# A fused attention, expert and gated layer: the last expert and the wide stage written out as one list of steps for three engines

## The chip, the core and the metric

The kernel runs on one core of a Trainium2 chip. Its engines work side by side, each on its own queue, in order: TensorE (PE in the profile; its weight loads are PEld), VectorE (DVE), ScalarE (ACT), GpSimd (POOL) and SyncE (SP), which here issues transfers. The metric is the device time of one execution in microseconds (us). The profile is that of one execution on this core.

## What is computed

Attention in a window of 128 positions gives 2304 tokens of 512 numbers. Each token goes to the one of eight experts that its gate picks (two layers, 512 to 1024 to 512). The result goes through a gated layer that all tokens share, 512 to 1536 to 512; this is the wide stage.

```
attn = softmax(scale*q@k.T + bias, inside a window of 128) @ v      # 4 batches, 8 heads, 576 positions
e_idx = argmax(x @ w_gate, axis=1)
for e in range(8):
    h = np.maximum(x[mask] @ w1[e], 0.0)
    out[mask] = gate_w[mask, None] * eom[mask, e, None] * (h @ w2[e])
g = x @ w_gate2;  val = x @ w_val                                   # x is now out
y = ((g * sigmoid(g)) * val) @ w_out
```

The weights of the gated layer come as 64-bit numbers and are narrowed to 32 bits in the kernel.

## The kernel before

Three stages follow each other: attention, the experts, the wide stage. A matmul takes 32-bit numbers as a high part and a low part (high = a rounded copy, written by ACT; low = number minus high, a subtraction by DVE or POOL), and every product is three passes: high by high, high by low, low by high (`PASSES`).

**Experts.** The experts are sorted by how many tokens they have; expert p takes `CAPS[p]` columns (384 for the first, 256 for the last two). Each has 16 steps: eight blocks `m` of the first layer, then eight blocks `kk` of the second. After every step `behind_step` turns some weights that will be needed later into high and low parts, by the table `plan`: rows of the next experts and, from step 40 on, halves of the wide stage's weights, which `narrow` puts together (two ACT operations, lines 327 and 329, then two DVE merges, lines 335 and 340). The results of an expert go to `ys`, a matrix in DRAM with one column for each token; they are copied by ACT and stored by transfers that ACT issues (`store_y`, for the seventh expert `store_whole`). The columns of `ys` that no expert may write are set to zero by four transfers in the attention stage (`zero_cols`, line 265).

**Wide stage.** The 2304 columns of `ys` are taken in three pairs of units (a unit is 384 columns), and each pair in 12 steps, one for each 128 columns of gate and value, so s runs from 0 to 35. A scheme with seven products in place of eight gives gate and value of both units: seven sums of the columns (`x_sum`, `x_high`, `x_low`) meet seven sums of the weights (`w_sum`, made by `sums`; `w_hi`; `w_lo`). In step s PE runs `product` 0 to 6, six matmuls of 384 columns each, into two banks `pa` and `pb`; and between them `wide_out(s - 2, ...)`, six groups of three matmuls of 512 columns, which multiply the finished activations of step s-2 with the output weights into six further banks. Beside PE, one step holds:

- ACT copies the banks (`s_p5`, `s_p1`, `s_u2`), two sigmoids, the high parts of the activations (`high`) and of the next step's weights (`w_hi`).
- DVE adds `v1`, `v2` and `g1` (lines 1377, 1395, 1408), multiplies (lines 1320, 1321, 1326, 1327), makes the low parts of the activations (`low`, line 1254) and three of the seven low parts of the weights (line 1080).
- POOL makes the other four low parts (line 1080) and the four sums of the weights (line 1063).

In the first pair, pair 0, each step also narrows two blocks of output weights (`out_weights`, `out_halves`: ACT, two merges each on DVE, the low parts on POOL, line 1303) and stores them to DRAM (`wo_s`), from which the later pairs load them again (`out_reload`). At the end of a pair the columns of the next are loaded (`load_unit`, line 967), summed (DVE and POOL, line 1027) and split (ACT line 1040, DVE line 1044), each 768 wide; and the finished rows of the pair leave by scatters that POOL issues (`wide_store`). For pair 0 this preparation lies in the steps of the last expert (`wide_early`).

What sets the order: inside `manual_schedule` every engine runs its instructions in the order in which the code issues them. So the loops above are the order. In a step of the wide stage the four merges stand on DVE ahead of `v2`:

```
if pr == 0:
    out_halves(G)
    out_weights(f)
TT(out=v2, in0=bank_a, in1=s_p5, op=ALU.add)
```

The seventh product adds into `bank_a`, so it waits until `v2` has read that bank. And at the end of the seventh expert:

```
if p == E - 2:
    for i in range(2):
        xraw[i] = new_slot((128, 2048), F32)
        load_unit(i)
...
store_whole(p, o, n)
```

The load of the first columns stands in front of the store of the seventh expert's results; the store goes to the same matrix at a column known only on the chip, and so waits until the load has landed, on ACT's queue.

Of the kernel before, what the change touches and what calls it, by code (L numbers as in the profile page):

```python
# [46 lines left out]
e2 E14.0 K13.1 r2 x11* S14.1 k2 D5 V12.0 H12 w2 H13 V12.1 D2 Q16.1 C14.1 H14 G5 v17 y0 y1 y2 y3 N5 p13.0 t7 M14.1 L11* l5 t4  # L47
# [5 lines left out]
x17 X15 L15* G8 X14 r4 a8 l8 a6 a7 k4 F8 D12 t17 f8 g5 D13 e5 w5 D15 r5 t16 b5 D14 X17 k5 X16 D17 D16  # L53
""".split()
# [3 lines left out]
def attn_moe_glu_kernel(ctx, tc, q, k, v, w_gate, w_ogate, w1, w2, w2_gate, w2_val, w2_out, out, caps=CAPS):  # L58
# [9 lines left out]
    WU = 384  # L68
# [56 lines left out]
    with ExitStack():  # L125
# [135 lines left out]
        LOW = caps[0] + min(caps)  # L261

        def zero_cols(d):
            w = next(x for x in range(RW, 0, -1) if (NT - LOW) % x == 0)
            nc.sync.dma_start(
                out=ys[d * 128:d * 128 + 128, LOW:NT].rearrange("p (a w) -> p a w", w=w),
                in_=zrow[:, 0:w].unsqueeze(1).to_broadcast([128, (NT - LOW) // w, w]),
            )

# [54 lines left out]
        def narrow(t, act=False, out=None):  # L324
# [3 lines left out]
            if act:  # L328
                nc.scalar.activation(  # L329
                    out=lo, in_=lo.bitcast(U32), func=AF.Copy, scale=2.0 ** -29 * (1 - 2.0 ** -11),  # L330
                    bias=2.0 ** -8 - 0.5,
                )
            else:
                nc.vector.tensor_scalar(out=lo, in0=lo, scalar1=29, scalar2=None, op0=ALU.logical_shift_right)
# [9 lines left out]

        loaded, halves, lows, n_rows = [], [], [], [0]
# [25 lines left out]
        def w_item(eng):  # L371
# [9 lines left out]
            else:  # L381
# [3 lines left out]
                narrow(t, True, wraw[fp][:, :, AT[name[0]][kk], :])  # L385
# [317 lines left out]
        def w_low(i):  # L703
# [5 lines left out]
            "q": load_qk, "v": load_v, "z": zero_fill, "y": zero_cols, "T": turn_in, "Q": keep_in, "S": scores, "C": select, "M": biased, "E": expo, "N": norm, "P": turn_p, "p": keep_p, "K": parts, "V": values, "x": keep_o, "t": turn_x, "X": rows_x, "D": place,  # L709
# [35 lines left out]
        tbl = wB[0].tile([128, 2048], F32, tag="wx", name="tbl", bufs=NX)  # L745

# [219 lines left out]
        def load_unit(u):  # L966
            nc.sync.dma_start(
                out=grid(xraw[u % 2], KD, WU), in_=ys[:, u * WU:u * WU + WU].rearrange("(k p) n -> p k n", p=128)
            )

# [12 lines left out]

        def store_whole(p, o, n):
            y = grid(raw_tile(), KD, n)
            for d in range(KD):
                nc.scalar.activation(out=y[:, d, :], in_=o[d][:, 0:n], func=AF.Copy)
            nc.scalar.dma_start(
                out=ys[:, bass.ds(off_reg[p], n)].rearrange("(k p) n -> p k n", p=128), in_=y
            )  # L990
# [18 lines left out]
        xset, wring, sbuf, wsum = [], [], [], []  # L1009
# [4 lines left out]
        def x_src(i):  # L1014
            r0, r1 = xraw
            return {0: sbuf[0], 1: r0[:, 0:UW], 2: sbuf[0], 3: sbuf[1], 4: sbuf[1], 5: r0[:, UW:2 * UW],
                    6: r1[:, UW:2 * UW]}[i] if sbuf else None

        def x_sum(i, eng):
            r0, r1 = xraw  # L1020
            a, b, op = {
                0: (r1[:, 0:UW], r1[:, UW:2 * UW], ALU.add),
                3: (sbuf[0], r0[:, 0:UW], ALU.subtract),
                2: (r0[:, UW:2 * UW], sbuf[1], ALU.subtract),
                4: (r0[:, 0:UW], r1[:, 0:UW], ALU.subtract),
            }[i]
            eng.tensor_tensor(out=x_src(i), in0=a, in1=b, op=op)
# [5 lines left out]
        def x_parts(i):  # L1033
            if i < 6:
# [3 lines left out]
        def x_high(i):  # L1038
            for src, hi, lo in x_parts(i):
                nc.scalar.activation(out=hi, in_=src, func=AF.Copy)  # L1040

        def x_low(i, eng):
            for src, hi, lo in x_parts(i):
                eng.tensor_tensor(out=lo, in0=src, in1=hi, op=ALU.subtract)
# [5 lines left out]
        def w_sum(s, i):  # L1050
# [3 lines left out]
        def sums(s, which):  # L1054
            if s >= NS:
                return
            g1, v2, g2, v1 = (w_raw(s, i) for i in range(4))
            for i in which:
                a, b, op = {
                    0: (v1, g1, ALU.subtract), 2: (v2, v1, ALU.subtract), 1: (w_sum(s, 2), g1, ALU.add),  # L1060
                    3: (g2, w_sum(s, 1), ALU.subtract),
                }[i]
                nc.gpsimd.tensor_tensor(out=w_sum(s, i), in0=a, in1=b, op=op)  # L1063

        def w_at(s, j):
            g = 7 * s + j
            return wring[g // 4 % 3][:, g % 4]

        def w_src(s, j):
            return w_sum(s, {0: 0, 3: 1, 4: 2, 6: 3}[j]) if j in (0, 3, 4, 6) else w_raw(s, {1: 0, 2: 1, 5: 2}[j])  # L1070

        def w_hi(s, *js):
            for j in js:
                if s < NS:
                    nc.scalar.activation(out=flat(w_at(s, j)[:, 0]), in_=w_src(s, j), func=AF.Copy)  # L1075

        def w_lo(s, eng, *js):
            for j in js:
                if s < NS:
                    eng.tensor_tensor(  # L1080
                        out=flat(w_at(s, j)[:, 1]), in0=w_src(s, j), in1=flat(w_at(s, j)[:, 0]), op=ALU.subtract
                    )

        def wide_early(i):
            def new(n, to, shape, dt=F32R):
                for _ in range(n):
                    assert wn[0] < freed[0] + NA + NBS
                    to.append(new_slot(shape, dt))

            V, G = nc.vector, nc.gpsimd  # L1090
            if i == 3:
                new(4, xset, (128, 2048))
                t = raw_tile()
                sbuf.extend(t[:, a * UW:a * UW + UW] for a in range(2))
                x_sum(0, V)
            elif i == 4:
                x_high(0)
                x_sum(3, V)
            elif i == 5:
                x_high(1)  # L1100
                x_low(0, V)
            elif i == 6:
                x_sum(2, G)
                x_high(3)
                x_low(1, V)
            elif i == 7:
                new(2, xset, (128, 2048))
                x_high(2)
                x_low(3, V)
                x_sum(4, G)  # L1110
            elif i == 8:
                x_high(4)
                x_low(2, V)
            elif i == 9:
                new(1, wsum, (128, 2048), F32)
                x_high(5)
                x_low(4, V)
            elif i == 10:
                x_high(6)
# [430 lines left out]
```

## Time and profile before

| | us |
|---|---|
| median of 3 runs (879.46 to 881.93) | 879.69 |
| the profiled execution | 881.72 |
| its span, first to last instruction | 879.9 |
| PE busy | 807.6 |
| DVE busy | 597.6 |
| ACT busy | 499.6 |
| POOL busy | 409.5 |
| mean granted TensorE clock | 0.971 |

Attention ends near 150 us, the experts take from there to 400 us, the wide stage the rest. A busy PE counts matmuls that overlap, so it does not show by itself how close PE is to its own pace; that is read from the distance of the starts in the timeline. Idle time is given with the instruction that ended it.

### The profile page before, as it was taken

How to read it: one execution, taken by the hardware profiler on the slowest of the kernel's cores; microseconds unless marked ns; L12 is line 12 of the kernel's file. 1: busy time of each engine (PE TensorE's matmuls, PEld its weight loads, DVE VectorE, ACT ScalarE, POOL GpSimd, SP SyncE). 2: the span in 40 equal slices, each digit the busy share in tenths (PEclk: the TensorE clock that was granted, in tenths of full speed). 3: DMA queues.
4: the chain of work that ended last, by engine and by line, in shares of the span. 5: the costliest groups of instructions: out<-in, count | busy, mean ns of one | idle time of the engine just before them, and what ended most of it. 6: DMA issues, size and time to landing. Idle time of an engine off the chain costs nothing. (4 is left out here: it accounts for less than half of the span.)

```text
span 879.9 us, 17654 instructions
## 1 busy us (share of the span) xinstructions
PE 807.6 (92%) x6111; PEld 738.8 (84%) x6111; DVE 597.6 (68%) x1429; ACT 499.6 (57%) x1355; POOL 409.5 (47%) x563
## 2 busy tenths in 40 slices
PE   8898998999999999986888988689999989999994
PEld 5787775899999999886777887689999878999993
DVE  7588988586667778847676667777555587655542
ACT  6798881355457767835655654455444456444441
POOL 5246795031222222307556556648555556755512
PEclk9999998999999999999999999799999999999998
DMA  9989963464568989940222421113131102211111
GB/s 189 238 219 282 236 240 134 161 222 158 182 193 292 293 280 285 295 171 13 72 85 96 134 82 61 48 49 121 48 120 46 45 30 90 79 39 36 48 49 74
DMA packets 115584, 121.66 MB, mean 138 GB/s; under 512 B 63266, under 2 KB 72482, under 8 KB 115490
## 3 DMA queue, kind: packets, MB, share of 16 engines
q1 hardware_dynamic: 106848, 105.76, 40.4%
q0 software_dynamic: 2880, 9.48, 2.8%
q10 hardware_dynamic: 5762, 5.25, 1.8%
q8 instruction: 49, 0.80, 0.4%
q14 instruction: 45, 0.37, 0.1%
HBM read 89.73 MB, written 30.73 MB: 137 GB/s over the span
## 5 line engine op out<-in xcount | busy, mean ns | idle before, releaser
L1241 PE MATMUL pa<-w 128*128 128x384 f32 x864 | 179.0, 343 | 27.0 <-DVE wtmp L1395 25.4
L1241 PEld LDWEIGHTS pa<-w 128*128 128x128 f32 x864 | 155.4, 191 | 43.4 <-DVE wtmp L1395 30.7
L1080 POOL TENSOR_TENSOR w<-w 128x256 fp32r<-128x256 f32 x105 | 77.7, 754 | 171.1 <-ACT w L1075 171.0
L1241 PE MATMUL pb<-w 128*128 128x384 f32 x648 | 135.9, 345 | 10.2 <-DVE wtmp L1408 4.0
L1265 PE MATMUL oo<-xh,hw 128*128 128x512 f32 x432 | 136.1, 397 | 0.0
L377 POOL TENSOR_TENSOR w<-raw,w 128x512 fp32r<-128x512 f32 x37 | 50.4, 1362 | 172.4 <-ACT w L375 114.9
L1241 PEld LDWEIGHTS pb<-w 128*128 128x128 f32 x648 | 117.5, 193 | 13.0 <-DVE wtmp L1408 5.0
L1189 PE MATMUL oy<-hh,w 128*128 128x384 f32 (+5 forms) x512 | 121.2, 316 | 5.1 <-DVE hl L1175 5.0
L1411 ACT ACTIVATE wtmp<-wtmp 128x384 f32<-128x384 f32 x36 | 18.9, 525 | 131.1 <-DVE wtmp L1408 131.1
L1189 PEld LDWEIGHTS oy<-hh,w 128*128 128x128 f32 x512 | 88.1, 191 | 5.9 <-DVE hl L1175 5.8
L1265 PEld LDWEIGHTS oo<-xh,hw 128*128 128x128 f32 x432 | 81.6, 192 | 6.9
L1265 PE MATMUL oo<-xl,hw 128*128 128x512 f32 x216 | 85.5, 396 | 1.6 <-POOL between L1282 1.6
L1164 PE MATMUL oh<-xh,w 128*128 128x384 f32 (+5 forms) x512 | 86.9, 308 | 0.0
L1189 PE MATMUL oy<-hl,w 128*128 128x384 f32 (+5 forms) x256 | 79.3, 310 | 0.0
L1164 PEld LDWEIGHTS oh<-xh,w 128*128 128x128 f32 x512 | 77.5, 188 | 0.5 <-ACT xh L959 0.4
L375 ACT ACTIVATE w<-raw 128x512 fp32r<-128x512 f32 x112 | 68.5, 627 | 9.0 <-ACT y L980 4.7
L1377 DVE TENSOR_TENSOR wtmp<-pb,wtmp 128x384 f32<-128x384 f32 x36 | 20.0, 555 | 61.5 <-ACT wtmp L1248 61.5
L190 POOL TENSOR_SCALAR_AFFINE_SELECT ptm<-pt 128x512 f32<-128x512 f32 x70 | 42.4, 634 | 40.8 <-ACT pt L418 40.0
L335 DVE SCALAR_TENSOR_TENSOR rawd<-rawd 128x256 int32<-128x256 int32 x72 | 46.7, 649 | 20.9 <-ACT rawd L329 16.8
L1248 ACT ACTIVATE wtmp<-pa 128x384 f32<-128x384 f32 x72 | 35.3, 490 | 45.0 <-PE pa L1241 44.8
L377 DVE TENSOR_TENSOR w<-raw,w 128x512 fp32r<-128x512 f32 x75 | 56.4, 758 | 3.2 <-ACT w L375 2.1
L1063 POOL TENSOR_TENSOR w<-wraw 128x256 f32<-128x256 f32 x72 | 57.1, 813 | 0.0
(249 smaller groups left out, 1669.6 us busy)
## 6 DMA issues: line engine op xcount, KB each, us to landing
raw<-in_moe_w_dram SPq DMA_DIRECT2D x128, 256.0 KB, 3.8
xs<-zrow SPq DMA_DIRECT2D x8, 774.0 KB, 5.9
rawd<-in_moe_w_gate_dram SPq DMA_DIRECT2D x24, 256.0 KB, 3.9
rawd<-in_moe_w_val_dram SPq DMA_DIRECT2D x24, 256.0 KB, 3.7
rawd<-in_moe_w_out_dram SPq DMA_DIRECT2D x24, 256.0 KB, 3.4
xh<-wo_s SPq DMA_DIRECT2D x24, 256.0 KB, 2.6
xl<-wo_s SPq DMA_DIRECT2D x24, 256.0 KB, 2.9
xr<-xs SPq DMA_DIRECT2D x6, 774.0 KB, 5.3
```

The lines of the kernel that those rows point to most:

```text
L190: nc.gpsimd.affine_select(out=o, in_=i, pattern=pat, compare_op=op, fill=fill, base=base, channel_multiplier=cm)
L335: nc.vector.scalar_tensor_tensor(out=lo, in0=hi, scalar=3, in1=lo, op0=ALU.logical_shift_left, op1=ALU.bitwise_or)
L375: nc.scalar.activation(out=s[:, 0, :], in_=t, func=AF.Copy)
L377: (nc.gpsimd if n_rows[0] % 3 == 0 else nc.vector).tensor_tensor(out=s[:, 1, :], in0=t, in1=s[:, 0, :], op=ALU.subtract)
L1063: nc.gpsimd.tensor_tensor(out=w_sum(s, i), in0=a, in1=b, op=op)
L1080: eng.tensor_tensor(out=flat(w_at(s, j)[:, 1]), in0=w_src(s, j), in1=flat(w_at(s, j)[:, 0]), op=ALU.subtract)
L1164: nc.tensor.matmul(out=o[:, 0:n], lhsT=wt["w1", p, m // 4, kk][:, a, (m % 4) * 128:(m % 4) * 128 + 128], rhs=(xh, xl)[b][:, kk, :], start= ...
L1189: nc.tensor.matmul(out=o[d][:, 0:n], lhsT=wt["w2", p, 0, kk][:, a, d * 128:d * 128 + 128], rhs=(hh, hl)[b][:, kk, :], start=(kk == 0 and i ...
L1241: nc.tensor.matmul(out=bank, lhsT=w[:, a, k, :], rhs=x_at(j, b, k), start=(start and n == 0), stop=(n == 5), skip_group_check=True,)
L1248: nc.scalar.activation(out=out, in_=in_, func=AF.Copy)
L1265: nc.tensor.matmul(out=o_w[c], lhsT=h_at(s, t)[b][:, b0 * 128:b0 * 128 + 128], rhs=wo_t[a][:, r * DM:r * DM + DM], start=(kk == 0 and i == 0),
L1377: TT(out=v1, in0=bank_b, in1=s_u2, op=ALU.add)
```

## The change

- `ORDER`: the four steps y0 to y3 (`zero_cols`) leave the attention stage. A tile of zeros, `zcols`, is set by POOL, and SP stores it to the same columns of `ys` in the steps 1, 3, 5 and 7 of the first expert.
- `plan`: the halves of the wide weights are spread over every second step from step 16 to 110, in place of two steps in three from 40 to 111.
- The loop over the experts ends after the seventh. The eighth, the preparation of pair 0 and all of the wide stage are issued by a list, `WIDE`, of some 3,000 steps, each a letter with numbers; `WSTEP` says which function a letter is. The list gives the order on PE, DVE, ACT, SP and POOL.
- All sums, differences and low parts of the wide stage are on DVE (`TT`); POOL keeps the scatters of `wide_store`.
- The results of the seventh and eighth expert are stored by SP (`store_6`, `result_7`); the load of the first columns (`load_pair`) is the first step of the list, and the loads of output weights begin after it (`wide_go`).
- `narrow` is cut in two steps, `narrow_act` (ACT) and `narrow_merge` (DVE), which the list places apart (X and Z); so are the copies and low parts of the output weights (p and z).
- The ring of high and low weights holds 11 blocks in place of 12.

```diff
+WIDE = """
+D0 A0 Y2 Y1 Y3 Y0 A1 r0 F q0 A2 r1 q1 A3 r2 q2 A4 r3 q3 h0.1 s0.0 A5 r4 s0.3 h0.0 A6 q4 r5 l0.0 A7 q5 r6 s0.2 q6 B0
...
+O1.0 d3.3 p2.0 f2 u4.1 P2.5 d3.6 w4.0 Z2.1 P2.6 u4.0 u4.2 g2 p2.1 O1.1 I2 d4.0 z2.0 P3.0 i2 J2 j2 P3.1 a3 K2 k2 M2
...
-            if st >= 40 and (st % 3 < 2 or st >= (E - 1) * STEPS) and left_h:
+            if st >= STEPS and st % 2 == 0 and left_h:
...
-                if name[1] > 0 and not sorted_known[0]:
+                if name[1] > 0 and not sorted_known[0] or name[0] == "o" and not wide_go[0]:
...
+        zcols = wB[0].tile([128, 2048], F32, tag="wx", name="zcols", bufs=NX)
+        nc.gpsimd.memset(zcols[:, 0:NT - LOW], 0.0)
...
-        def store_whole(p, o, n):
-            y = grid(raw_tile(), KD, n)
-            for d in range(KD):
-                nc.scalar.activation(out=y[:, d, :], in_=o[d][:, 0:n], func=AF.Copy)
-            nc.scalar.dma_start(
-                out=ys[:, bass.ds(off_reg[p], n)].rearrange("(k p) n -> p k n", p=128), in_=y
-            )
...
+            TT(out=x_src(i), in0=a, in1=b, op=op)
...
-                nc.gpsimd.tensor_tensor(out=w_sum(s, i), in0=a, in1=b, op=op)
...
+            TT(out=w_sum_at(s, i), in0=a, in1=b, op=op)
...
+        def w_lo(s, j):
+            TT(out=flat(w_at(s, j)[:, 1]), in0=w_src(s, j), in1=flat(w_at(s, j)[:, 0]), op=ALU.subtract)
...
+        def store_6():
+            n = caps[PL - 1]
+            nc.sync.dma_start(
+                out=ys[:, bass.ds(off_reg[PL - 1], n)].rearrange("(k p) n -> p k n", p=128), in_=last["y6"]
+            )
...
+        def out_merge(s, c):
+            last["f", s, c] = narrow_merge(*last.pop(("n", s, c)))
...
+            TT(out=wo_at(s, 1, c * 256, 256), in0=last.pop(("f", s, c)), in1=wo_at(s, 0, c * 256, 256), op=ALU.subtract)
...
+            "A": last_l1, "r": last_relu, "q": last_low, "B": last_l2, "Y": result_6, "F": store_6, "y": result_7,
+            "D": load_pair, "s": x_sum, "h": x_high, "l": x_low, "w": w_sum, "u": w_hi, "d": w_lo,
+            "P": product, "O": wide_out, "E": wide_store, "W": out_reload,
+            "X": out_narrow, "Z": out_merge, "p": out_high, "z": out_low,
...
+                    if p == 0 and m % 2:
+                        d = m // 2
+                        nc.sync.dma_start(out=ys[d * 128:d * 128 + 128, LOW:NT], in_=zcols[:, 0:NT - LOW])
...
+            for step in WIDE:
+                WSTEP[step[0]](*(int(x) for x in step[1:].split(".") if x))
+                if step == "D0":
+                    wide_go[0] = True
+                    w_load()
```

What the list moves on the engines shows at two places. First, DVE in step 4 of the wide stage, before: `v1` (line 1377), the four merges, then `v2` (1395), `g1` (1408) and the products of gate and sigmoid.

```order
L1377 TENSOR_TENSOR wtmp<-pb,wtmp 128x384
L335 SCALAR_TENSOR_TENSOR rawd<-rawd 128x256
L340 SCALAR_TENSOR_TENSOR rawd<-rawd 128x256
L335 SCALAR_TENSOR_TENSOR rawd<-rawd 128x256
L340 SCALAR_TENSOR_TENSOR rawd<-rawd 128x256
L1395 TENSOR_TENSOR wtmp<-pa,wtmp 128x384
L1408 TENSOR_TENSOR wtmp<-pb,wtmp 128x384
L1320 TENSOR_TENSOR wtmp<-wtmp 128x384
```

The same step on DVE now; line 1344 is `v1`, `v2` and `g1` in turn, 412 and 417 are the merges, 1177 a low part and 1156 a sum of the weights, 1341 a product.

```order
L1344 TENSOR_TENSOR wtmp<-pb,wtmp 128x384
L1177 TENSOR_TENSOR w<-w 128x256 x2
L412 SCALAR_TENSOR_TENSOR rawd<-rawd 128x256
L417 SCALAR_TENSOR_TENSOR rawd<-rawd 128x256
L1344 TENSOR_TENSOR wtmp<-pa,wtmp 128x384
L1156 TENSOR_TENSOR w<-wraw 128x256
L1344 TENSOR_TENSOR wtmp<-pb,wtmp 128x384
L412 SCALAR_TENSOR_TENSOR rawd<-rawd 128x256
L417 SCALAR_TENSOR_TENSOR rawd<-rawd 128x256
L1341 TENSOR_TENSOR wtmp<-wtmp 128x384
```

One pair of merges has moved from ahead of `v2` to behind `g1`, and work that was POOL's stands between. The second place is SP's queue at the end of the seventh expert, before: `rawd` with `val` is the last of the wide weights, with `out` the output weights, `w<-ys` the load of the first columns, `wo_s` the first store of output weights.

```order
L359 DMA rawd<-in_moe_w_val_dram 128x512 x2
L359 DMA rawd<-in_moe_w_out_dram 128x512 x7
L967 DMA w<-ys 128x4x384 x2
L1306 DMA wo_s<-xh 128x512
L1306 DMA wo_s<-xl 128x512
```

And now; `ys<-xr` is the store of the seventh expert, `ys<-y` the first of the eighth.

```order
L444 DMA rawd<-in_moe_w_val_dram 128x512
L1242 DMA w<-ys 128x4x384 x2
L444 DMA rawd<-in_moe_w_out_dram 128x512 x7
L1231 REGISTER_ALU
L1231 DMA ys<-xr 128x4x256
L1227 REGISTER_ALU
L1227 DMA ys<-y 128x256
```

The load of the columns now stands ahead of the seven loads of output weights, and the store of the seventh expert, once on ACT's queue, stands behind both on SP's.

## Rows read from the trace of the kernel before

**Rows 1.** The page, part 1: engine, busy us, share, instructions.
```profile
PE 807.6 (92%) x6111; PEld 738.8 (84%) x6111; DVE 597.6 (68%) x1429; ACT 499.6 (57%) x1355; POOL 409.5 (47%) x563
```

**Rows 2.** Stretches of the wide stage: us, then busy us of PE, PEld, DVE, ACT, POOL.
```profile
401.68:415.78 14.10, 8.52 (x36) 7.55 (x36) 12.32 (x20) 7.31 (x22) 10.97 (x13) 0.88 0.06 19
415.78:427.61 11.83, 8.20 (x43) 7.13 (x43) 8.96 (x17) 7.57 (x21) 6.33 (x9) 1.00 0.17 59
427.61:442.18 14.57, 13.29 (x60) 11.98 (x61) 9.23 (x17) 7.78 (x21) 8.45 (x12) 0.88 0.28 95
442.18:546.71 104.53, 93.67 (x481) 85.15 (x481) 70.09 (x129) 60.18 (x160) 61.92 (x81) 1.00 0.27 91
546.71:569.86 23.15, 14.91 (x61) 12.86 (x61) 18.42 (x22) 10.55 (x24) 13.34 (x12) 0.76 0.13 45
569.86:585.09 15.23, 14.57 (x61) 13.28 (x62) 11.03 (x18) 7.74 (x18) 6.38 (x9) 0.81 0.00 2
700.00:722.00 22.00, 17.29 (x82) 15.14 (x81) 19.27 (x23) 9.36 (x21) 13.62 (x13) 0.93 0.15 48
```

**Rows 3.** Waits of PE from 340 us on: us in total, times, longest.
```profile
PE pa L1241 <- DVE wtmp L1395: 25.4, 13, 6.5
```

**Rows 4.** Timeline of PE, seventh and eighth expert: start, us, instruction, idle before.
```profile
358.53 0.39 PE L1189 MATMUL oy<-hh,w 128*128 128x256 f32 x1 [1.13 <-DVE hl L1175]
...
386.98 0.38 PE L1189 MATMUL oy<-hh,w 128*128 128x256 f32 x1 [3.87 <-DVE hl L1175]
...
394.15 0.40 PE L1189 MATMUL oy<-hh,w 128*128 128x256 f32 x2
...
394.50 0.40 PE L1189 MATMUL oy<-hh,w 128*128 128x256 f32 x2
...
399.80 0.28 PE L1189 MATMUL oy<-hh,w 128*128 128x256 f32 x1
```

**Rows 5.** Timelines of SP and ACT in the eighth expert.
```profile
369.33 1.23 SPq L359 DMA_DIRECT2D rawd<-in_moe_w_val_dram  x2
...
376.58 1.19 SPq L967 DMA_DIRECT2D w<-ys  x2
...
386.08 1.49 ACT L1172 ACTIVATE hh<-oh 128x256 fp32r<-128x256 f32 x5 [9.82 <-DMA w<-ys]
```

**Rows 6.** Timeline of a step of pair 1, PE and DVE.
```profile
621.30 1.22 PE L1241 MATMUL pa<-w 128*128 128x384 f32 x6
...
622.03 0.56 DVE L1320 TENSOR_TENSOR wtmp<-wtmp 128x384 f32<-128x384 f32 x1 [0.65 <-ACT wtmp L1411]
...
622.36 1.21 PE L1241 MATMUL pb<-w 128*128 128x384 f32 x6
...
624.21 1.23 DVE L1254 TENSOR_TENSOR hw<-wtmp,hw 128x384 fp32r<-128x384 f32 x2
...
625.37 0.42 DVE L1080 TENSOR_TENSOR w<-w 128x256 fp32r<-128x256 f32 x1
...
625.70 0.42 DVE L1080 TENSOR_TENSOR w<-wraw,w 128x256 fp32r<-128x256 f32 x1
...
632.76 1.22 PE L1241 MATMUL pa<-w 128*128 128x384 f32 x6
```

**Rows 7.** Timeline of a step of pair 0, DVE, POOL and PE.
```profile
503.91 0.43 DVE L335 SCALAR_TENSOR_TENSOR rawd<-rawd 128x256 int32<-128x256 int32 x1 [0.73 <-ACT rawd L329]
...
504.91 1.79 POOL L1063 TENSOR_TENSOR w<-wraw 128x256 f32<-128x256 f32 x2
...
505.15 0.96 DVE L335 SCALAR_TENSOR_TENSOR rawd<-rawd 128x256 int32<-128x256 int32 x1
...
...
507.50 1.31 PE L1241 MATMUL pa<-w 128*128 128x384 f32 x6 [1.36 <-DVE wtmp L1395]
```

**Rows 8.** Timeline of DVE between pair 0 and pair 1.
```profile
575.77 0.96 DVE L1044 TENSOR_TENSOR w<-xr,w 128x768 fp32r<-128x768 f32 x1 [0.17 <-ACT w L1040]
```

**Rows 9.** Timeline of PE, the seventh product of step 34.
```profile
847.06 1.22 PE L1241 MATMUL pa<-w 128*128 128x384 f32 x6
```

**Rows 10.** The first expert: us, busy us of the engines, clock, DMA share, GB/s.
```profile
150.00:200.00 50.00, 50.00 (x291) 45.02 (x290) 32.91 (x84) 20.33 (x40) 8.59 (x6) 1.00 0.58 191
```

More of the change, by code (lines that the diff above doesn't have):

```diff
@@ new lines, in result_6, with result_7 @@
+        def result_6(d):
+            n = caps[PL - 1]
+            if "y6" not in last:
+                last["y6"] = grid(raw_tile(), KD, n)
+            copy(last["y6"][:, d, :], last["o6"][d][:, 0:n])
+        def result_7(d):
+            n = caps[PL]
+            y = s_p.tile([128, CP], F32, tag="sc", name="y")[:, 0:n] if d < 2 else (
+                sbuf[0][:, 2 * UW + (d - 2) * n:2 * UW + (d - 2) * n + n])
+            copy(y, last["y"][d][:, 0:n])
+            nc.sync.dma_start(out=ys[d * 128:d * 128 + 128, :][:, bass.ds(off_reg[PL], n)], in_=y)
@@ new lines, in product, with high, low @@
+        def product(s, j):
+            w = w_at(s, j)
+            n = 0
+            for a, b in PASSES:
+                for k in range(2):
+                    nc.tensor.matmul(
+                        out=bank_of(j), lhsT=w[:, a, k, :], rhs=x_at(j, b, k), start=(n == 0 and j in (0, 1, 5)),
+                        stop=(n == 5), skip_group_check=True,
+                    )
+                    n += 1
+        def high(s, t):
+            copy(h_at(s, t)[0], temp(6 + t))
+        def low(s, t):
+            TT(out=h_at(s, t)[1], in0=temp(6 + t), in1=h_at(s, t)[0], op=ALU.subtract)
@@ new lines, in wo_at, with wide_out @@
+        def wo_at(s, i, a=0, n=DM):
+            if not wo_t:
+                wo_t.extend(pair_tile(xe_p, "x", KD * cap))
+            return wo_t[i][:, s % 3 * DM + a:s % 3 * DM + a + n]
+        def wide_out(s, c):
+            if c not in o_w:
+                o_w[c] = ps_m.tile([128, DM], F32, tag="m", name="oo")
+            t, b0 = divmod(c, WB)
+            kk = s % KF2
+            for i, (a, b) in enumerate(PASSES):
+                nc.tensor.matmul(
+                    out=o_w[c], lhsT=h_at(s, t)[b][:, b0 * 128:b0 * 128 + 128], rhs=wo_at(s, a),
+                    start=(kk == 0 and i == 0), stop=(kk == KF2 - 1 and i == 2),
+                )
@@ new lines, in wide_store @@
+        def wide_store(pr, c):
+            ob = stg.tile([128, DM], F32, tag="stg", name="ob")
+            if pr == NP - 1:
+                copy(ob[:, 0:DM // 2], o_w[c][:, 0:DM // 2])
+                nc.vector.tensor_copy(ob[:, DM // 2:DM], o_w[c][:, DM // 2:DM])
+            elif c % 2:
+                nc.vector.tensor_copy(ob, o_w[c])
+            else:
+                copy(ob, o_w[c])
+            nc.gpsimd.memset(between, 0.0)
+            r = nc.gpsimd.indirect_dma_start(
+                out=out[:, :], out_offset=bass.IndirectOffsetOnAxis(ap=oid[:, 2 * WB * pr + c, :], axis=0),
+                in_=ob, in_offset=None,
+            ).ins
+            tc.declare_no_dep(r, group="out", reason="every row is written once")
+            tc.add_to_no_dep_group("out", r)
@@ new lines, in out_narrow, with out_high, out_low @@
+        def out_narrow(s, c):
+            name, kk, c_, t = loaded.pop(0)
+            assert name[0] == "o" and (kk, c_) == (s, c)
+            halves.append(t)
+            last["n", s, c] = narrow_act(t)
+        def out_merge(s, c):
+            last["f", s, c] = narrow_merge(*last.pop(("n", s, c)))
+        def out_high(s, c):
+            copy(wo_at(s, 0, c * 256, 256), last["f", s, c])
+        def out_low(s, c):
+            TT(out=wo_at(s, 1, c * 256, 256), in0=last.pop(("f", s, c)), in1=wo_at(s, 0, c * 256, 256), op=ALU.subtract)
+            halves.pop(0)
+            if c:
+                for i in range(2):
+                    nc.sync.dma_start(out=wo_s[i, s * 128:s * 128 + 128, :], in_=wo_at(s, i).bitcast(F32))
+            w_load()
@@ L1154, in attn_moe_glu_kernel @@
             tokens = token_order()
-            for p in range(E):
+            for p in range(E - 1):
                 n = caps[p]
```

550 lines of the change are left out of this document (240 added, 310 removed).

## The prediction

> **What bounds the kernel now.** I read the page first: PE is busy 92% of the span [rows 1]. That is a mean over stages, so the next view is the table of stretches. In the first expert PE is busy in every microsecond [rows 10]; in the wide stage it is not: 93.67 of 104.53 us in steps 3 to 10, 14.91 of 23.15 at the turn to pair 1, 8.52 of 14.10 in step 0 [rows 2]. The third view, PE's waits by releaser, names one cause for most of it: `v2` on DVE (line 1395), which the seventh product waits for, 25.4 us in 13 waits [rows 3]. The fourth is the timeline, which gives the pace without waits. In a step of pair 1 the seventh product starts at 621.30 and the next step's at 632.76, a period of 11.46 us; the product after it starts at 622.36, so a product is 1.06 us (1.05 below), and the six groups of `wide_out` are (11.46 - 7 x 1.05) / 6 = 0.69 us each [rows 6]. PE is the bound there, and this change leaves PE's matmuls as they are, and from step 3 on their order too. What can be won is the difference between the wide stage as it runs and 11.46 us a step, and the same for the last expert.
>
> **What PE loses now.** The edges of [rows 2] are the starts of the seventh product of steps 0, 1, 2, 10, 11 and 12. The eighth expert ends at 399.80 + 0.12 = 399.9 [rows 4]. Without waits the seventh product of step 0 would start six products later, at 406.2; it starts at 415.78: 9.6 us lost. Steps 0 and 1 have no `wide_out`, so step 1 needs 7.35 and takes 11.83: 4.5. Step 2 needs 11.46 and takes 14.57: 3.1. Steps 3 to 10 take 104.53 where 8 x 11.46 = 91.7 would do: 12.9, or 1.6 a step. Step 11: 11.7; step 12: 3.8. From there to the seventh product of step 34, at 847.06 [rows 9], it is 261.97 us for 22 steps, which need 252.1: 9.9, nearly all of it around the turn to pair 2, where PE is busy 17.29 of 22.0 us [rows 2]. Sum 55.5 us. What lower granted clocks (0.76 and 0.81 at the first turn, 0.88 in step 0) cost is inside these numbers, since they are distances of starts.
>
> In the last two experts there is a wait of 1.13 us, one of 3.87 us, and after it a slow stretch: from 386.98 to 399.9 the second layer takes 12.9 us, where 32 groups of three matmuls at the 0.35 us of 394.15 to 394.50 need 11.3 [rows 4]. Sum 1.1 + 3.9 + 1.6 = 6.6 us.
>
> So the floor of this change, with PE never waiting from the eighth expert on, is 881.7 - 55.5 - 6.6 = 819.6 in the profiled execution.
>
> **The change part by part.**
>
> *Eighth expert.* ACT stood 9.82 us behind the load of the columns, because the store of the seventh expert waited for it on ACT's queue; the late high parts are the 3.87 us of PE [rows 4, 5]. The store is on SP now and nothing that ACT runs stands behind it. The load moves ahead of seven loads of output weights. It was issued at 376.58 and had landed when ACT went on at 386.08 [rows 5], some 9 us; ahead of the seven it can go as soon as the last wide weights are issued, which was at 369.33 [rows 5]; I take 366 to 372, and land it at 375 to 381. Behind it SP holds the seven loads, the two kinds of stores and the next columns' load, which nothing needs before step 12. The 6.6 us go.
>
> *Start of the wide stage.* Before the eighth expert's end DVE has to do four sums and six low parts 768 wide at 0.96 [rows 8], two more low parts 384 wide at 0.56, and some eleven operations on the first weights at 0.33: 14.4 us. From 375 this ends at 389.4, from 381 at 395.4, and the expert ends at 399.9 - 6.6 = 393.3. Steps 0 and 1 then ask as much of DVE as of PE: by the prices of the next part 7.9 and 9.5 us, against 7.35 and 9.4 of PE, which now begins `wide_out` of step 0 in step 1. Of the 9.6 + 4.5 + 3.1 us lost, I leave 3 standing; bounds 0 (all hidden) and 13 (the load lands as late as now).
>
> *Steps 2 to 12.* DVE takes over POOL's work and is asked for 26 operations in a step: 17 that are 256 wide (seven low parts, four sums, two low parts of output weights, four merges) and 9 that are 384 wide. Back to back, 256-wide ones start 0.33 us apart (625.37, 625.70); four 384-wide ones from 622.03 to 624.21 take 0.55 each [rows 6]; a merge that needs the one before it a little more, which I take as 0.46. Together 15 x 0.33 + 2 x 0.46 + 9 x 0.55 = 10.8 us of 11.46. So DVE fits, with 0.6 us to spare. What made PE wait, four merges between `v1` and `v2`, is down to two, and these have 2.4 us of PE's work (two groups of `wide_out` and the fifth product) to hide in. I walked one step through in the new order with these prices, and no wait of PE is left. The merges themselves get shorter: line 335 takes 0.43 us with POOL still and 0.96 beside POOL's sums [rows 7], and POOL runs only scatters here now. The bounds are PE's pace (all 12.9 us go) and every operation at its full length alone, 17 x 0.43 + 9 x 0.56 = 12.35 us a step, 0.9 over PE's, through steps 2 to 15: 12.5 us left. The row of back-to-back starts is the nearer one, since the list sets operations side by side that don't need each other. I leave 3.
>
> *The turns.* Preparing a pair is eleven DVE operations 768 wide, 10.5 us at 0.96 [rows 8], now spread over steps 8 to 12 and 17 to 24 and paid with low parts of weights made earlier or later. At the first turn DVE's sum over the steps is at most PE's less 0.3 us a step; at the second there are no merges and DVE has 3 us to spare a step. Of 11.7 + 3.8 + 9.9 us lost I leave 2; bounds 0 and 10.
>
> *Zeros, table of weights.* The zeros move from a time at which SP had nothing else to do to the first expert, 3.4 MB (4 x 128 rows x 1664 columns x 4 bytes) beside a DMA share of 0.58 and 191 GB/s [rows 10]; there they stand ahead of weight rows in SP's queue, which are needed some steps later. Cost 0, bounds 0 and 4. In the attention stage nothing waited for them: 0, gain at most 1. The wide weights, spread from step 16 on, fall into experts in which PE never waits: 0.
>
> **Sum.** 881.7 - 6.6 - 55.5 + 3 + 3 + 2 = 827.6 us in the profiled execution, which is 2.0 us above the median of the runs. So the median should go from 879.7 to 825.6; I say 826.
>
> [...]
>
> **Rivals.**
>
> *DVE becomes the bound in pair 0.* For it: 95% of DVE's time is spoken for, and each step has two places where DVE must wait for a copy by ACT. Against: the starts 0.33 us apart. Price: 12.5 us in steps 2 to 15 in place of 3, and 6 at the turns in place of 2: 839. Then PE waits a little in every step to 15 and not after.
>
> *The start is not won.* The columns land when they did, because the load waits for a slot or a store that the rows don't show. Then the 6.6 us of the expert go all the same, but step 0 begins near 402 as now: 13 us in place of 3, 836.
>
> *The order does not hold what it says.* One instruction out of place on an engine's queue keeps a wait in every step of pair 0 and the turns as they are: only the expert and half of the start go, 881.7 - 6.6 - 9 - 2 = 864.
>
> *Slower: DVE pays POOL's price.* If a 256-wide operation with two inputs in SBUF is slow for another reason than POOL's traffic (0.96 us was seen [rows 7]), then DVE sets the step: at 0.9 us it needs 17 x 0.9 + 5.0 = 20.3 us in pair 0 and 11 x 0.9 + 5.0 = 14.9 later, so 13 x 8.8 + 23 x 3.4 = 193 us over PE's pace: about 1010. It is slower than before from a mean of 0.61 us on (13 x 3.9 + 23 x 0.3 = 58 us). Against it: the same operations take 0.42 with PE and ACT at work and POOL still [rows 6]. [...]
>
> **How the numbers follow.** The forecast, PE back as the bound with 2 to 16 us of waits left, 818 to 832: 62%. DVE the bound in pair 0, 833 to 845: 20%. The start not won, 833 to 838: 10%. The order failing, about 864: 4%. Slower by DVE's price: 3%. No change to speak of: 1%. The range goes from 816, the floor less the 2.0 us and a little for the attention stage, to 846, where the first two rivals end; outside are some 10%. Within 0.3% (2.6 us) a measurement of this kernel can't tell a change. Faster 0.95, the same 0.02, slower 0.03.
>
> **What would show it.** In the changed kernel's profile: POOL, busy 61.92 us in steps 3 to 10 [rows 2], is busy for under 1 us a step in the wide stage, and DVE for 10 or more in steps 2 to 12; the wait of ACT for the load of the columns is gone, and the eighth expert's second layer starts with no gap; the seventh products of steps 3 to 10 stand 11.5 us apart; line 412 (the old 335) is 0.43 us in every step; the first turn costs PE under 3 us. It would be wrong if the steps of pair 0 stand 12 us or more apart (first rival), if step 0 begins later than 397 (second), if 256-wide operations on DVE last over 0.6 us with POOL still (the last), or if PE waits in the experts that had no wait.

## The result and the profile after

The changed kernel takes 827.6 us (median of 4 runs, 825.66 to 828.42) against 879.6 in the same session, a ratio of 0.940 with a 95% interval of 0.938 to 0.943. The prediction was 826. Its profiled execution took 828.4 us, its span 826.7.

The page's first part, engines with busy time, share of the span and instructions, against [rows 1]:

```profile
PE 790.8 (96%) x6111; PEld 731.7 (88%) x6111; DVE 657.4 (80%) x1745; ACT 504.4 (61%) x1353; POOL 160.8 (19%) x250
```

The same stretches as in [rows 2], cut at the starts of the seventh product: from the eighth expert's end to step 0, step 1, step 2, steps 3 to 11, step 12. Columns: stretch, its length, busy us of PE, PEld, DVE, ACT, POOL, granted clock, DMA share, GB/s.

```profile
389.83:396.93 7.10, 6.52 (x38) 6.20 (x37) 7.04 (x21) 6.47 (x21) 0.00 (x0) 1.00 0.11 37
396.93:417.40 20.47, 12.31 (x52) 11.12 (x52) 10.37 (x27) 8.21 (x22) 0.00 (x0) 0.76 0.45 142
417.40:427.67 10.27, 10.27 (x56) 9.80 (x55) 8.95 (x23) 6.53 (x18) 0.00 (x0) 0.98 0.30 102
427.67:530.14 102.47, 102.47 (x538) 96.07 (x538) 96.92 (x235) 69.41 (x172) 0.00 (x0) 1.00 0.24 80
530.14:541.60 11.46, 11.46 (x61) 10.74 (x60) 11.20 (x26) 8.31 (x20) 0.00 (x0) 1.00 0.58 184
```

From step 2 on PE is busy in every microsecond, at the pace of 11.46 us a step (step 3 takes 10.75), through the first turn and the second, whose rows are not printed here. DVE is busy for 96.92 / 9 = 10.8 us a step. One stretch is bad: step 1 takes 20.47 us. All of PE's waits from 340 us on, in place of [rows 3]:

```profile
PE pa L1268 <- ACT wtmp L1129: 8.5, 2, 7.9
PE pa L1268 <- DVE wtmp L1341: 0.3, 1, 0.3
```

Who makes ACT late shows in the timelines of SP, ACT and PE around it (start, length, engine, instruction, in brackets the idle time before and what ended it):

```profile
365.01 0.98 SPq L1242 DMA_DIRECT2D w<-ys  x2
366.10 6.50 SPq L444 DMA_DIRECT2D rawd<-in_moe_w_out_dram  x7
374.40 0.42 SPq L1231 DMA_DIRECT2D ys<-xr  x1
...
396.64 0.37 SPq L444 DMA_DIRECT2D rawd<-in_moe_w_out_dram  x1
...
400.31 0.95 SPq L1242 DMA_DIRECT2D w<-ys  x2
401.30 0.51 SPq L1330 DMA_DIRECT2D wo_s<-xh  x1
401.85 0.62 SPq L1330 DMA_DIRECT2D wo_s<-xl  x1
402.52 0.43 SPq L444 DMA_DIRECT2D rawd<-in_moe_w_out_dram  x1
```

```profile
410.95 0.43 ACT L405 ACTIVATE rawd<-rawd 128x256 f32<-128x256 f32 x1 [8.30 <-DMA rawd<-in_moe_w_out_dram]
...
411.60 0.47 ACT L1129 ACTIVATE wtmp<-pa 128x384 f32<-128x384 f32 x1
```

```profile
401.67 1.21 PE L1268 MATMUL pa<-w 128*128 128x384 f32 x6
...
412.12 2.29 PE L1268 MATMUL pa<-w,w 128*128 128x384 f32 x6 [7.88 <-ACT wtmp L1129]
```

Two more views tell what the second `w<-ys` did to SP's queue: what SP itself waited for between 395 and 415 us, and the time from issue to landing of the halves issued between 395 and 420 us.

```profile
SPq L1242 <- DMA ys<-w: 2.6, 1, 2.6
DMA to landing us min/median/max: 3.2/3.2/8.3
```

The first load is as hoped: the columns go at 365.01, ahead of the seven loads of output weights, and the store comes behind on SP (in [rows 5] they went at 376.58). At 400.31 the same kind of load fetches the second pair's columns (1.5 MB). Behind it, at 402.52, goes the ninth half of the output weights; ACT stands 8.30 us for it with the copy of `pa` queued behind, and PE stands 7.88 us for that copy. The load of the columns delays the half twice: it holds SP's queue for 2.6 us, since it reads the matrix into which the eighth expert's results are still being stored, and the half then takes 8.3 us to land, where the others take 3.2. The product that follows takes 2.29 us in place of 1.21: PE had stood still for 7.88 us, and the granted clock is 0.50 from 412 to 417 us.

### The profile page after: what moved, and what is told of

It is laid out like the page before. It is cut to its first block, busy times and chain, and to the rows that moved or that the text cites. A ratio compares the mean times of both kernels' runs of the same rounds, so it can differ in the third digit from the quotient of the medians.

```text
span 826.7 us, 17558 instructions
## 1 busy us (share of the span) xinstructions
PE 790.8 (96%) x6111; PEld 731.7 (88%) x6111; DVE 657.4 (80%) x1745; ACT 504.4 (61%) x1353; POOL 160.8 (19%) x250
## 3 DMA queue, kind: packets, MB, share of 16 engines
q1 hardware_dynamic: 106416, 106.81, 43.8%
## 5 line engine op out<-in xcount | busy, mean ns | idle before, releaser
L1268 PE MATMUL pa<-w 128*128 128x384 f32 x630 | 127.8, 338 | 0.9 <-ACT wtmp L1129 0.6
L1268 PEld LDWEIGHTS pa<-w 128*128 128x128 f32 x630 | 112.3, 188 | 9.3 <-ACT wtmp L1129 0.9
L1306 POOL DMA_INDIRECT out_dram<-ob,oid x18 | 17.8, 991 | 432.9 <-ACT ob L1129 306.8
L1268 PE MATMUL pb<-w 128*128 128x384 f32 x468 | 94.4, 336 | 0.0
L1268 PEld LDWEIGHTS pb<-w 128*128 128x128 f32 x468 | 82.8, 188 | 0.3
L1129 ACT ACTIVATE w<-w 128x256 fp32r<-128x256 f32 (+2 forms) x168 | 75.8, 460 | 10.5 <-DVE w L1156 7.3
L1344 DVE TENSOR_TENSOR wtmp<-pb,wtmp 128x384 f32<-128x384 f32 x72 | 40.1, 556 | 40.9 <-ACT wtmp L1129 34.7
L1129 ACT ACTIVATE w<-wraw 128x256 fp32r<-128x256 f32 x108 | 44.3, 413 | 41.9 <-PE pa L1268 25.8
L1341 DVE TENSOR_TENSOR wtmp<-wtmp 128x384 f32<-128x384 f32 x108 | 58.6, 554 | 6.4 <-ACT wtmp L1347 5.8
L576 ACT ACTIVATE p<-p,mn 128x128 f32<-128x128 f32 x144 | 55.8, 397 | 1.1 <-DVE mn L555 1.1
```

The costliest lines, as they stand in the source:

```text
L576: last_exp[0] = nc.scalar.activation(out=pr[:, c, :], in_=pr[:, c, :], func=AF.Exp, bias=mn[:, c:c + 1], scale=-1.0, accum_out=sums[j][:, ...
L1129: nc.scalar.activation(out=out, in_=in_, func=AF.Copy)
L1268: nc.tensor.matmul(out=bank_of(j), lhsT=w[:, a, k, :], rhs=x_at(j, b, k), start=(n == 0 and j in (0, 1, 5)), stop=(n == 5), skip_group_che ...
L1306: r = nc.gpsimd.indirect_dma_start(out=out[:, :], out_offset=bass.IndirectOffsetOnAxis(ap=oid[:, 2 * WB * pr + c, :], axis=0), in_=ob, in_ ...
L1341: TT(out=out, in0=a, in1=b, op=ALU.mult)
L1344: TT(out=temp(i), in0=bank_of(j), in1=temp(k), op=ALU.add)
```

## Experiments

The theory: the order of the list (it has 1,928 steps, not some 3,000), which keeps what PE waits for ahead of what it does not, made the gain in pair 0 and at the turns; the eighth expert's gap was the store on ACT's queue; what is left is SP's queue. The main rival: POOL's absence did it, since its work stretched DVE's.

**The second load moved.** One word of the list goes from step 1 to step 5:

```diff
-... f0 u2.1 D1 z0.1 ...
+... f0 u2.1 z0.1 ...
-c5 d6.3 O3.4 ...
+c5 D1 d6.3 O3.4 ...
```

> Step D1, the load of the second pair's columns (1.5 MB), goes from step 1 of the wide stage to step 5. Theory: PE's last stall of the changed kernel (7.88 us in step 1, with some 2.5 us of lower clock behind it) is ACT waiting for the ninth half of the output weights, which lands late because SP issues that load behind D1. Then the 8.30 us wait of ACT shrinks to under 2 us, the stall of PE to under 1.5, and the median falls from 827.6 to 817 to 820 us. Rival: the half is late because its buffer comes free only then, or because of the two stores of weights that stand ahead of it too; then the load is issued some 2 us earlier and no more, ACT still waits 4 to 6 us, and the median is 823 to 826.

Measured: 818.7 us (816.34 to 822.0), ratio to before 0.929 (0.926 to 0.933), clear of the changed kernel's 0.938 to 0.943. PE's longest item of waits from 340 us on, then steps 0 and 1:

```profile
PE pa L1268 <- ACT wtmp L1129: 0.6, 1, 0.6
```

```profile
393.72:401.13 7.41, 6.83 (x38) 5.98 (x37) 7.38 (x22) 6.89 (x23) 0.00 (x0) 1.00 0.11 36
401.13:411.25 10.12, 9.84 (x53) 9.02 (x53) 9.87 (x26) 7.71 (x21) 0.00 (x0) 1.00 0.42 131
```

Step 1 takes 10.12 us for 20.47, and the clock stays at 1.00. From the first product to the end of the span it is 426.6 us (820.3 - 393.72) for 436.9. The ninth half goes 9.0 us after the first product (402.70), where it went 12.7 us after it, and the halves now land in 3.3 to 3.9 us. So the load's place in SP's queue was the cause, and neither the buffer nor the two stores: they stand as before. This kernel beats both. (Its profiled execution entered the first expert 3.9 us later than the changed kernel's, so its stretches lie later.)

**POOL back, in the new order.**

```diff
-            TT(out=w_sum_at(s, i), in0=a, in1=b, op=op)
+            nc.gpsimd.tensor_tensor(out=w_sum_at(s, i), in0=a, in1=b, op=op)
...
+            e = nc.gpsimd if j > 2 else nc.vector
+            e.tensor_tensor(out=flat(w_at(s, j)[:, 1]), in0=w_src(s, j), in1=flat(w_at(s, j)[:, 0]), op=ALU.subtract)
...
+            nc.gpsimd.tensor_tensor(
```

The last line is the low part of the output weights. The sums of the columns (`x_sum`), which POOL shared with DVE before, stay on DVE.

> The changed kernel in its own order, with the four sums of weights, four of the seven low parts and the low parts of the output weights on POOL again. If the order of the list alone made the gain in pair 0 and at the turns, the time stays within 3 us of the changed kernel: 825 to 831. If it was the engine (POOL's operations of 0.9 us stretch DVE's merges from 0.43 to 0.96 and the products wait for low parts), the steps of pair 0 stand 12.5 us apart or more again and the time is 840 to 850. I expect a value near the upper end of the first: POOL has 7.7 us of work in a step of 11.46.

Measured: 842.3 us (841.14 to 843.5), between the two. Where the 14.7 us lie, in stretches with the columns as above (seventh products of steps 2 to 9, then of 9 to 16), and in DVE's merges between 420 and 540 us (busy us, mean ns):

```profile
433.35:513.10 79.75, 79.75 (x418) 74.49 (x418) 68.36 (x116) 53.22 (x141) 60.83 (x74) 1.00 0.29 92
513.10:601.55 88.45, 83.27 (x421) 74.13 (x420) 71.03 (x110) 47.77 (x113) 63.20 (x78) 1.00 0.24 82
```

```profile
L417 DVE SCALAR_TENSOR_TENSOR rawd<-rawd 128x256 int32<-128x256 int32 x18 | 15.3, 851 | 0.6
L412 DVE SCALAR_TENSOR_TENSOR rawd<-rawd 128x256 int32<-128x256 int32 x18 | 12.5, 696 | 0.0
```

Through steps 3 to 9 PE never waits, with POOL busier than in [rows 2] (60.83 of 79.75 us for 61.92 of 104.53) and the merges long again (0.70 and 0.85 us, for 0.42 and 0.43 in the changed kernel): there the order alone is enough. POOL costs at the turn (88.45 us where 7 x 11.46 = 80.2 would do, 8.2 lost) and at the start: from the first product to the seventh of step 2 it is 43.8 us for the changed kernel's 37.8. There DVE's 768-wide sums stand beside POOL's work (at the turn six of them take 1.29 us each for 0.95), and ACT, for whose copies PE waits, waits for POOL's sums of the weights. ACT's longest item between 513.10 and 601.55:

```profile
ACT w L1129 <- POOL w L1156: 10.9, 7, 2.4
```

So both halves of the change earn, in different places.

**The merges moved as a block, in the kernel before.**

```diff
-                if pr == 0:
-                    out_halves(G)
-                    out_weights(f)
                 TT(out=v2, in0=bank_a, in1=s_p5, op=ALU.add)
...
                 TT(out=g1, in0=bank_b, in1=s_p1, op=ALU.add)
+                if pr == 0:
+                    out_halves(G)
+                    out_weights(f)
```

> The kernel before with one thing changed: in pair 0 the block that narrows the output weights (its copies, its four merges on DVE, its low parts on POOL) is issued behind v2 and g1 and not ahead of v2. POOL keeps its work. If the order of DVE's queue was the cause of the 1.6 us lost in each step of pair 0, the seventh products of steps 3 to 10 come to 11.5 to 11.8 us apart and the time falls by 10 to 13 us, to 867 to 870; start, turns and the eighth expert stay as they are. If it was POOL's work beside DVE (merges of 0.96 us, products that wait for low parts), the merges only delay the products of gate and sigmoid instead, and the time stays within 5 us of 879.7.

Measured: 872.5 us, ratio 0.990 (0.986 to 0.993): 8 us for the 10 to 13 expected. Steps 4 to 10 are 12.7 to 12.8 us apart for 13.07, so neither the 11.5 to 11.8 of the one theory nor no change. In the profiled executions, 8.3 us apart, 3.1 come from steps 3 to 10 and 2.4 from the first turn; 3.3 are there by the seventh product of step 0, and 1.0 of these by the first product, ahead of which nothing was changed. The wait of [rows 3] on `v2` has turned into another:

```profile
PE pa L1241 <- DVE wtmp L1326: 11.0, 11, 2.1
```

Line 1326 is the gate's product, now queued behind the four merges, and it too stands before a bank that PE wants. Four merges in one block stalled PE at both places that were tried; the list sets two and two, with other work between.

**The engine alone, in the kernel before.**

```diff
-        V, G = nc.vector, nc.gpsimd
+        V, G = nc.vector, nc.vector
...
-                nc.gpsimd.tensor_tensor(out=w_sum(s, i), in0=a, in1=b, op=op)
+                nc.vector.tensor_tensor(out=w_sum(s, i), in0=a, in1=b, op=op)
```

> The kernel before with its order as it is, and the sums, differences and low parts of the wide stage on DVE instead of POOL (the other half of the change alone). If the engine was the cause, the merges get short (0.43) and steps 3 to 10 come close to 11.5 us: 862 to 868. If the order was, v2 now stands behind eight more DVE operations, four merges and three or four low parts, and the seventh product waits for it as long or longer: 878 to 900. After the run with POOL back in the new order I expect the second, near 885.

Measured: 887.0 us, ratio 1.006 (1.003 to 1.009): 0.6% slower, small but clear of the noise. Steps 5 to 10 are 13.54 to 13.58 us apart, and outside the turns the steps of pairs 1 and 2 go from 11.46 to some 11.7. PE's waits:

```profile
PE pb L1241 <- DVE wtmp L1408: 16.6, 16, 2.6
PE pa L1241 <- DVE wtmp L1395: 15.8, 13, 3.6
```

The merges are short here (0.42 and 0.43 us between 440 and 550) and PE waits all the same. DVE has room for POOL's work in the sum and not in the old order. The half of the change that looks like its substance makes the kernel slower by itself.

**Only the eighth expert's fix, in the kernel before.**

```diff
-                if name[1] > 0 and not sorted_known[0]:
+                if name[1] > 0 and not sorted_known[0] or name[0] == "o" and not wide_go[0]:
...
-            nc.scalar.dma_start(
+            nc.sync.dma_start(
...
                         load_unit(i)
+                    wide_go[0] = True
+                    w_load()
```

> The kernel before with three edits at the eighth expert: the seventh expert's results are stored by SP and not by ACT, that expert's column is read into a register of SP, and the first loads of output weights are issued behind the load of the columns. The prediction's terms say that the 6.6 us of the last two experts go and a part of the start's 9.6 us: 866 to 873. If the expert's gap came from something else than the store on ACT's queue, the time stays near 879.

Measured: 876.7 us, ratio 0.996 (0.993 to 0.999): 3.8 us, less than expected. The end of the expert and the first products:

```profile
392.76 0.28 PE L1190 MATMUL oy<-hh,w 128*128 128x256 f32 x1
397.61 1.65 PE L1244 MATMUL pb<-w 128*128 128x384 f32 x4 [4.57 <-ACT w L1076]
401.32 1.01 PE L1244 MATMUL pb<-w 128*128 128x384 f32 x2 [2.06 <-DVE w L1081]
```

The expert ends at 392.9 for 399.9 [rows 4], 7.0 us earlier; 0.8 of it was there when the seventh expert's second layer began (355.97 for 356.78), so the edit made 6.2 where 6.6 were forecast. Then PE waits for the first pair's high and low parts, which are made in the old order on DVE and POOL, and the first product comes 4.1 us earlier (397.61 for 401.68): 2.9 are given back. A gain ahead of a stage stays only if that stage's preparation is ready too.

**The first load's place.** First the gate on the output weights' loads was opened (`wide_go = [True]`).

> The changed kernel with the first seven loads of output weights issued when buffers come free, so ahead of the load of the first columns again, as in the kernel before; the store of the seventh expert stays on SP. By the prediction's bound the columns land about 9 us later (near 381 instead of 374), DVE starts its 14.4 us of preparation that much later, and PE waits in steps 0 and 1: 3 to 9 us more, 831 to 837. Rival: the wait of the old kernel was only the store on ACT's queue, and the place of the load among SP's costs nothing: 827 to 829.

Measured: 827.5 us (826.81 to 828.77), and it tells nothing of the place: the load still went at 364.38 and 365.47, with one of the seven between. So the load was put behind them in the list:

```diff
-D0 A0 Y2 Y1 Y3 Y0 A1 r0 F q0 A2 r1 q1 A3 r2 q2 A4
+A0 Y2 Y1 Y3 Y0 A1 r0 F q0 A2 r1 q1 A3 r2 q2 D0 A4
```

> The changed kernel with the load of the first columns behind the seven loads of output weights and behind the store of the seventh expert, as the kernel before had it behind the seven loads; the run before this in which only the gate was taken away left the load where it was. The columns then land some 9 to 11 us later, near 385. By the prediction's bound (13 us lost at the start if the columns land as late as in the kernel before) the time is 833 to 841. If DVE has room enough in the eighth expert, 827 to 829.

Measured: 836.2 us (832.97 to 838.97), 8.6 more than the changed kernel. SP, and what DVE waits for:

```profile
365.75 5.48 SPq L444 DMA_DIRECT2D rawd<-in_moe_w_out_dram  x7
371.42 0.42 SPq L1231 DMA_DIRECT2D ys<-xr  x1
377.62 0.94 SPq L1242 DMA_DIRECT2D w<-ys  x2
```

```profile
384.26 1.95 DVE L1114 TENSOR_TENSOR w<-w 128x768 f32<-128x768 f32 x2 [9.32 <-DMA w<-ys]
```

Issued 12.6 us later, the columns cost 8.6 us: the eighth expert hides only the rest. The seven loads make up about half of the 12.6: behind them the load also waits 5.7 us for the store to land, which in the kernel before stood behind it.

**How much room DVE has.** Four additions that nothing needs, in each of steps 2 to 10:

```diff
+                if step[0] == "c" and 2 <= int(step[1:]) <= 10:
+                    extra()
```

`extra` issues the four, each on 256 columns of scratch.

> Four additions of 256 columns on DVE, on numbers that nothing needs, are added to each of the steps 2 to 10, behind the copy of the second sum of the fourth product. By the prediction's price of a step (10.8 of 11.46 us spoken for) the four need 1.3 to 1.7 us where 0.6 is free: each of nine steps gets 0.7 to 1.1 us longer, the time 834 to 838, and the steps stand 12.2 to 12.6 us apart. If DVE's slack is larger than the rows of starts say, nothing changes: 827 to 829.

Measured: 834.5 us (833.21 to 835.22), 6.9 more. Steps 4 to 10 stand 12.06 to 12.75 us apart, and PE waits for DVE where it never did:

```profile
PE pb L1268 <- DVE wtmp L1344: 3.9, 9, 1.0
```

```profile
446.02 1.80 DVE L1453 TENSOR_TENSOR w<-w 128x256 f32<-128x256 f32 x4
447.74 0.42 DVE L1156 TENSOR_TENSOR w<-wraw,w 128x256 f32<-128x256 f32 x1
```

Each of the four needs the one before, so together they take 1.7 us (446.02 to 447.74) and not four times 0.33; steps 3 to 10 are 0.9 us longer each. That leaves some 0.8 us of room in a step, where the rows of starts said 0.6.

**The same four on POOL.** `nc.vector` in `extra` becomes `nc.gpsimd`.

> The same four additions on the same numbers at the same place as in the run with four more DVE operations in steps 2 to 10 (which cost 0.9 us a step, 834.5 in all), but on POOL, which has nothing else to do there. If a POOL operation that reads two inputs in SBUF holds up DVE's operations beside it, as the two lengths of line 335 in [rows 7] suggest, then DVE's operations of 0.42 us show lengths near 0.9 while POOL runs, DVE's sum goes over PE's 11.46 us, and the four cost about as much as they did on DVE: 832 to 838. If the long merges of the kernel before had another reason than POOL's traffic, DVE's lengths stay and the time is 827 to 829.

Measured: 834.5 us (833.62 to 836.8). Nothing holds POOL back, so it ran all 36 in one go early, not four a step:

```profile
402.56 32.02 POOL L1453 TENSOR_TENSOR w<-w 128x256 f32<-128x256 f32 x36 [32.87 <-ACT w L1129]
```

DVE's operations while POOL runs, and, behind the dots, after it has ended at 434.6:

```profile
414.96 0.95 DVE L1156 TENSOR_TENSOR w<-wraw 128x256 f32<-128x256 f32 x1
415.83 0.95 DVE L412 SCALAR_TENSOR_TENSOR rawd<-rawd 128x256 int32<-128x256 int32 x1
...
418.05 0.56 DVE L1344 TENSOR_TENSOR wtmp<-pb,wtmp 128x384 f32<-128x384 f32 x1
...
435.59 0.41 DVE L1156 TENSOR_TENSOR w<-wraw 128x256 f32<-128x256 f32 x1
435.93 0.41 DVE L412 SCALAR_TENSOR_TENSOR rawd<-rawd 128x256 int32<-128x256 int32 x1
...
436.72 0.55 DVE L1344 TENSOR_TENSOR wtmp<-pb,wtmp 128x384 f32<-128x384 f32 x1
```

The price is as expected and its place is not: all of it falls ahead of the seventh product of step 2. The lengths settle the disputed point: 0.41 becomes 0.95 beside POOL, on numbers that have nothing to do with POOL's. That the median is 834.5 on either engine is chance, as the time is lost in different steps.

**The old spread of the wide weights.**

```diff
-            if st >= STEPS and st % 2 == 0 and left_h:
+            if st >= 40 and (st % 3 < 2 or st >= (E - 1) * STEPS) and left_h:
```

> The changed kernel with the old rule for the wide weights (two steps in three from step 40 on). The prediction puts the new spread at nothing: 827 to 829. If the spread is what lets the load of the first columns go at 365 and the eighth expert start without the wait of 1.13 us, the time is 829 to 832.

Measured: 834.6 us (832.88 to 836.06), 7 more than the changed kernel, above both expectations. The profiled execution runs with the changed kernel's to 356.2 us. It loses 2.8 us from there to the first product (392.73 for 389.83) and 3.0 more to the seventh product of step 0 (the load of the first columns goes at 367.56 for 365.01, and PE waits for ACT); 1.5 of this comes back, so its span is 4.4 us longer. ACT at the head of the eighth expert still narrows wide weights:

```profile
375.24 0.44 ACT L405 ACTIVATE rawd<-rawd 128x256 f32<-128x256 f32 x1 [2.58 <-DMA rawd<-in_moe_w_val_dram]
...
375.90 0.64 ACT L1129 ACTIVATE xr<-oy 128x256 f32<-128x256 f32 x2
```

```profile
392.73 0.88 PE L1268 MATMUL pb<-w,w 128*128 128x384 f32 x4
...
397.29 0.45 PE L1268 MATMUL pb<-w,w 128*128 128x384 f32 x1 [1.72 <-ACT wtmp L1129]
```

The copies of the seventh expert's results stand behind ACT's wait. The seventh expert's second layer takes 13.9 us and the eighth's two layers 11.3 each, where the changed kernel has 11.9, 10.9 and 10.9. The profiled executions are the fastest of this kernel and the slowest of the changed one, so they show 4.4 of the 7 us and no more.

## Why the prediction was right, and where it was lucky

- *PE is the bound, 11.46 us a step.* Right: from step 3 to 34 the seventh products stand 11.46 to 11.48 us apart. From the first product to the seventh of step 34 the need was 6.3 + 7.35 + 33 x 11.46 = 391.8 us; it takes 403.9 (12.1 more), and 393.7 with the second load moved.
- *Eighth expert, 6.6 us.* Right: 6.2 when only that was changed. Of its terms, the 1.6 us of slow second layer are for the most part the clock: behind the wait of 3.87 us the clock granted to the kernel before was 0.51 for 3.4 us, as this row of it shows (columns as in [rows 2]); its 18 matmuls need 2.1 us at the distances of [rows 4]. With only the eighth expert's fix PE does not wait there, and the layer takes 11.5 us (381.37 to 392.9) for 12.9. So the wait cost more than its own length.

```profile
388.00:391.40 3.40, 3.40 (x18) 3.40 (x17) 2.60 (x5) 1.61 (x3) 0.00 (x0) 0.51 0.05 16
```

- *Zeros, 0.* Nothing speaks against it (PE is busy without a gap from 150 to 390 us); they were not tried alone.
- *The spread of the wide weights, 0.* Wrong: it is worth 4 to 7 us. The prediction looked at the idle rows of the experts that get more work and not at the ones that are relieved: the seventh expert's second layer took 14.3 us before (356.78 to 371.07) and takes 11.9, where the prediction had counted a wait of 1.1; the eighth's first layer took 12.0 beside its wait of 3.87 and takes 10.9. Most of that shows in no row of waits. Part of it is PE's pace: three matmuls of 256 columns, 0.35 us apart in [rows 4], are 0.34 apart in the changed kernel's eighth expert (below), at a granted clock of 1.00 in both, which is 0.8 us over its two layers. With the old spread the layers take 11.3 us each, the old pace; what in the spread sets the pace no run shows. So the eighth expert ends at 389.8, where 393.3 was forecast, 3.5 us better: 2.8 of them in these three layers (the eighth's second layer gives the last 0.5), and 0.7 ahead of them, of a cause that no run shows.

```profile
386.66 0.39 PE L1209 MATMUL oy<-hh,w 128*128 128x256 f32 x2
...
387.00 0.39 PE L1209 MATMUL oy<-hh,w 128*128 128x256 f32 x2
```

- *Start, 3 us left.* Mis-sized: with pair 0 and the turns 8 us were left standing, and 12.1 were (403.9 - 391.8), 10.2 of them by the second load. The step that failed is the sentence on SP's queue: behind the first load SP holds, among others, "the next columns' load, which nothing needs before step 12". It is not needed early, but what stands behind it is. The prediction asked when each transfer is needed and not what it delays, for a queue of which it had named the content. What it delayed is measured: 2.6 us in which the load held the queue, and a landing of 8.3 us for 3.2.
- *Pair 0, 3 us, and the turns, 2.* Both cost nothing: DVE's 10.8 us of 11.46 was right, and the list uses it to the end. Of the two reasons given, the merges' place carries steps 3 to 9; their shorter length is not needed there, and POOL's silence pays at the start and the turns. The prediction had credited both to the same steps. It also read the 0.43 us of line 335 in [rows 7] as taken with POOL still. This row of the kernel before has POOL at work beside it, in its two low parts until 504.95; merges with POOL still are seen in the changed kernel (0.42 and 0.43 us).

```profile
503.27 1.68 POOL L1303 TENSOR_TENSOR xl<-rawd,xh 128x256 fp32r<-128x256 f32 x2
```

- *Rivals.* DVE does not become the bound in pair 0, but four more operations a step make it so. The start not won cost 8.6 us when the load was put later, for the 10 that the rival added; that the total of 836.2 meets the 836 forecast is luck, as it holds the second load's stall, which the rival did not have. DVE at POOL's price does not come, as POOL is still (the merges take 0.42 and 0.43 us).

So the waits left standing were put 4.1 us too low and the experts' gain 3.5 too low. The two nearly cancel: that 826 came so near 827.6 is luck, while the mechanism stands.

## What to carry to other kernels

A change of order and a change of engine that come together should be priced apart: here the engine alone is a loss (0.6%), the new order with most of POOL's work left on POOL keeps some 37 of the 52 us, and the rest appears only with both. For every transfer that a change moves in an issue queue, ask what is queued behind it and when that is needed; a large early load ahead of a small urgent one cost 10 us of PE's time here, and 8.9 of the median. And look for time lost without a wait, by comparing the length of equal stages (two second layers of the same size), not by the rows of waits alone.

## What the runs showed of the hardware

In the run with the four additions on POOL, which each have two inputs in SBUF, DVE's operations of lines 1156 and 412 (128x256, two SBUF inputs) took 0.95 us beside POOL and 0.41 after it, while those with one input in PSUM (line 1344, 128x384) took 0.56 and 0.55. The same width with both inputs in SBUF took 1.09 beside POOL, where the changed kernel's mean is 0.55 (line 1341):

```profile
418.05 0.56 DVE L1344 TENSOR_TENSOR wtmp<-pb,wtmp 128x384 f32<-128x384 f32 x1
...
420.15 1.09 DVE L1341 TENSOR_TENSOR wtmp<-wtmp 128x384 f32<-128x384 f32 x1
```

Work given to POOL was thus not cheaper here: the same 36 additions cost 6.9 us on either engine. Not every DVE operation with two SBUF inputs beside POOL was long: in the kernel before line 335 took 0.43 us from 503.91 [rows 7], while the second of POOL's two low parts took 0.97 us, for 0.75 of the first.
